# Alternating column halves in the last heads' values, 28 masks on ACT, tau loaded apart, and a new plan

## The chip, the cores and the metric

The kernel runs on one core of a Trainium2 chip. The metric is the device time of one execution in microseconds. The engines are named as in the profile: PE (TensorE; PEld is its weight load), DVE (VectorE), ACT (ScalarE), POOL (GpSimd) and SP (SyncE, which issues DMAs here).

## The reference

An attention with a threshold, then two feed-forward layers on its output. Attention has 4 batches, 8 heads, 576 positions and 64 columns a head; each layer has 2304 tokens, 512 columns and 2048 inner columns.

```python
scores = scale * np.matmul(q, k.transpose(0, 1, 3, 2))
thresh = np.max(scores, axis=-1, keepdims=True) - tau
scores = np.where(scores >= thresh, scores, -1000000000.0)
scores = scores - np.max(scores, axis=-1, keepdims=True)
attn = np.exp(scores)
attn = attn / (np.sum(attn, axis=-1, keepdims=True) + 1e-09)
return np.matmul(attn, v).astype(np.float32)
...
r = np.maximum(h, 0.0)      # first layer: g = r * r, h = x @ w_in
g = h * np.tanh(sp)         # second layer: sp = log(1 + exp(h))
return (g @ w_out).astype(np.float32)
```

The weights of both layers come as 64-bit floats, which the kernel reads as pairs of 32-bit words.

## The kernel before, in words

The work is a list of operations (`op`, `dma`), each with the engines that may do it, an estimated duration on each, what it reads and writes, and a due time. `Plan.order` then lays them out with a model of the engines (`forwards`, `backwards`), and the kernel is issued in the order of the starts that this gives. The table `PAR` holds the due times and the choices of buffers; `LOADS` holds the estimated issue and transfer times of each kind of DMA. What an engine does, and in which order, is therefore fixed before the run; on the chip each engine takes its own list in order and waits on semaphores.

Attention goes through the 4 batches in turn, each as 4 pairs of heads. A pair has 576 query positions: four units of 128 queries with two heads each (`hh` 0 and 1), and a last unit of 64 queries, in which the two heads share the 128 partitions (`hh` = 2: head 0 in partitions 0 to 63, head 1 in 64 to 127). A unit computes scores on PE (`unit`, `scores`), on DVE the scaled scores with their minimum (`top`, L882), the threshold (`most`, L892), on ACT the exponential (`weigh`, L908), and on DVE the mask (`mask`, L919), which multiplies the exponentials with "score within the threshold" and sums them up in `l`. So nine heads are weighed a pair, if the last unit counts as one. Then the weights are turned and multiplied with the values.

There are kinds of pairs. Kind d (all four of batch 0, one of batch 1) works in float32: PE turns the weights (`values_direct`, L991), ACT copies them out, PE multiplies (two heads alternate in `turned`; the last unit's `values` does one head after the other). Kinds h and s (the other 11 pairs) split the weights into two f16 parts, turn them by DMA (`transpose`, tile pt), and multiply with two f16 parts of the values in `values` of `head`, L956 to L962: 14 matmuls a head.

Weights of the first layer (`weights`) are rewritten to two float32r parts each: on ACT a scaling (L525), on ACT or DVE a shift of the lower word (L537 or L544), on DVE a clamp (L532) and two bit operations (L549, L555), the upper part on ACT or DVE (L583), the lower part on DVE (L594). This runs beside the attention of batches 0 and 1, in places of buffers that the planner lends. The first layer's blocks (`first_part`: tiles h and acc) run between the units of later batches; the second layer comes last.

At the start one operation, `consts`, makes the identity, loads tau and does three small DVE operations with it; everything that reads the identity or these numbers depends on it in the plan. `warm` puts single 128-column matmuls (`spin`) into PE's early idle time, in three groups.

Of the kernel before, what the change touches and what calls it, by code (L numbers as in the profile page):

```python
# [16 lines left out]
AF = mybir.ActivationFunctionType  # L17
ALU = mybir.AluOpType
# [8 lines left out]
PAR = dict(  # L27
    on=dict(),
    merge=8,
    warm=(1, 3, 7),  # L30
    won=("S", "S"),
    land=2.419,
    lag=0.518,
    turns=("h", "s1"),
    kv=(("nat0", "V1"), ("f1", "nat1"), ("KT1", "f0"), ("V0", "KT0")),
    cd=(-150.532, 10.911, -114.568),
    urg=-5.54,
    rawt=23.548,
    kinds="dddd",
    cgen=1.383,  # L40
    split=(),
    ex=dict(cw=1, cr=6, raw=17, pd=2, sc=3),
    exo=("cw", "pd", "sc", "cr", "raw"),
    blk=list((17.026, 77.25, 181.004, 262.558, 368.796, 471.734, 577.967, 790.694, 936.347)),
    tb2=145.883,
    down2=89.229,
    sp=(0, 0),
    off=(170.46, 68.826, 37.695, -205.928, 58.656, 43.101, -191.105, -38.461),
    ahead=(10.872, 128.518, 9.367, -61.853, 3.491, 155.716, -16.749, 483.826, 162.488, -31.72),
    start=-197.714,  # L50
    area=dict(sc=("x0", "x1"), hl=("x2",)),
    jobahead=19.381,
    fbi=6,
    stay=1.0,
    stayt=150.0,
    kinds2="ssss",
    kb=("dhss", "ssss", "ssss"),
)

# [21 lines left out]
class Plan:  # L81
# [5 lines left out]
    TABLE = 1.3  # L87
    BIAS = {"V": 1.26, "A": 0.34, "P": 3.463, "S": 0.46}
    SHARE = 0.8
# [238 lines left out]
def attention_moe_moe_kernel(ctx: ExitStack, tc: tile.TileContext, q, k, v, tau, w1i, w1o, w2i, w2o, out):  # L328
    nc = tc.nc
    B, H, S, D = q.shape  # L330
# [3 lines left out]
    plan = Plan()  # L334
    op = plan.op
# [68 lines left out]
    def rot(*places):  # L404
# [9 lines left out]
        "q1": (dict(S=0.75, P=0.8), 0.0, 0.4, 0.4), "q2": (dict(S=1.45, P=1.4), 0.62, 0.19, 0.65),  # L414
        "w8": (dict(S=0.65, P=0.9, A=0.5), 0.0, 3.5, 3.45),
        "w": (dict(S=0.6, P=0.75, A=0.45), 0.0, 1.8, 1.75), "n3": (dict(S=2.3, P=2.0), 1.24, 0.9, 1.6),
        "n2": (dict(S=1.45, P=1.35), 0.62, 0.5, 1.4),
        "xs": (dict(S=0.72, P=0.65), 0.0, 0.36, 0.36), "tail": (dict(S=1.6, P=1.3), 0.6, 0.19, 0.38),
        "xl": (dict(S=0.63, P=0.56), 0.0, 0.55, 0.5), "x2": (dict(S=0.6, P=0.56), 0.0, 0.75, 0.7),
        "xr": (dict(S=0.45, P=0.56), 0.0, 0.64, 0.64), "out": (dict(S=0.45, A=0.45), 0.0, 0.65, 0.65),  # L420
        "out2": (dict(S=1.3), 0.6, 0.2, 0.5), "turn": (dict(S=1.55), 0.0, 1.3, 1.2),
    }
# [11 lines left out]
    def mm(o, l, r, start, stop):  # L434
        nc.tensor.matmul(o, l, r, start=start, stop=stop, skip_group_check=True)  # L435
# [11 lines left out]

    K, K0 = plan.buf("const", lambda: None), plan.buf("ones", lambda: None)
    op({"P": 0.5}, lambda e: nc.gpsimd.memset(ones, 1.0), w=[K0], due=-60.0)

    def consts(e):
        make_identity(nc, ident)
        nc.sync.dma_start(out=tt[:, 3:4], in_=tau.to_broadcast([128, 1]))

        nc.vector.tensor_scalar(
            out=tt[:, 0:1], in0=tt[:, 3:4], scalar1=0.0, scalar2=-0.125, op0=ALU.is_ge, op1=ALU.mult
        )
        nc.vector.tensor_scalar(out=tt[:, 1:2], in0=tt[:, 3:4], scalar1=0.0, scalar2=None, op0=ALU.max)

        nc.vector.tensor_copy(out=cd[:, 3:4], in_=tt[:, 0:1])  # L460

    op({"S": 0.5}, consts, w=[K], due=-50.0, load=(0.0, 0.7, 0.7))


    W = {}
# [159 lines left out]
    def pow2(name, raws, junk, due):  # L625
# [23 lines left out]
        t = pbuf(place("s", "s0", "s1"), [128, 1024])  # L649
        op({"T": 0.22}, lambda e: mm(t()[:, 0:n], ones, mx(), True, True), r=[mx, K], w=[t], due=due + 0.1)  # L650

# [104 lines left out]
    turns = []  # L756
# [17 lines left out]
    def job_direct(p, due):  # L774
# [10 lines left out]
        for x, dst, z, (j0, j1) in todo:  # L785
# [23 lines left out]

            t = op({"T": 0.15 * (j1 - j0)}, turn, r=[raw, K], w=[o], due=due - z)  # L810
            if len(turns) < 2:
# [33 lines left out]
    def unit(p, g, hh, j, due):  # L845
# [9 lines left out]
        def scores(e):  # L855
# [13 lines left out]

        op({"T": (1.2 if direct else 0.85) if hh < 2 else 0.65 if direct else 0.48}, scores, r=[QT, KT], w=ss, due=due,  # L870
           half=3 if direct else 2)
# [33 lines left out]
    def weigh(p, hh, j, i, sc, m, nt, due):  # L905
        ex = sbuf(place("e", "e0", "e1"), [128, 576], F32)
        op({"A": 0.67},
           lambda e: nc.scalar.activation(  # L908
               out=ex(), in_=sc(), func=AF.Exp, bias=m()[:, i:i + 1], scale=-1.0),
           r=[sc, m], w=[ex], due=due + 1.5 - URG, tab=("exp", "ln"))  # L910
# [12 lines left out]

        op({"V": 0.74}, mask, r=[sc, nt], x=[ex], w=[l], due=due + 2 - URG, two=True)

        return u, ex

    def head(p, g, hh, u, ex, due):
# [26 lines left out]
        def values(e):  # L955
            for h in ((hh,) if hh < 2 else (0, 1)):  # L956
                sl = slice(0, 128) if hh < 2 else slice(64 * h, 64 * h + 64)
                for i in range(9):
                    t = 5 * h + (i if i < 5 else i - 5)
                    mm(o()[sl, 64 * u:64 * u + 64], pt()[:, i, sl], V()[:, t, 0:64], i == 0, i == 8)  # L960
                    if i < 5:
                        mm(o()[sl, 64 * u:64 * u + 64], pt()[:, i, sl], V()[:, t, 64:128], False, False)  # L962

        op({"T": 0.41 if hh < 2 else 0.9}, values, r=[pt, V], w=[o], due=due + 7 + O_VA, half=1)
        if last:
            normal(p, g, hh, due)

    def values_direct(p, g, hh, u, ex, last, o, due):
# [23 lines left out]

        op({"T": 0.6}, turn, r=[ex, K], w=ts, due=due + 2.5 + O_DIR)
        if not p.late:
# [115 lines left out]
    def attention(b, groups, t0, t1, tails):  # L1110
        n = NPR * (4 * len(groups) + tails)
        i = 0
        for pr in range(NPR):
# [62 lines left out]
    def x_first(n, due):  # L1176
        xh, xo = sbuf("xh", [128, 2, 4, 128], F32R), sbuf("xo", [128, 2, 4, 128], F32R)
        o = pbuf(rot("s0", "s1"), [128, 1024])
        for t in range(2):
            for g in range(2):  # L1180
# [315 lines left out]
```

## Time and profile before

| | us |
|---|---|
| median of 3 runs | 1029.93 (1028.37 to 1031.53) |
| the profiled execution | 1031.52 |
| its span | 1029.7 |
| PE busy | 1002.4 |
| DVE busy | 617.9 |
| ACT busy | 622.0 |

The span runs from the first to the last instruction; the rest of an execution's time lies around it. Busy time of PE is by modelled ends, since matmuls are pipelined. The page's second part cuts the span into 40 equal slices; a digit is the busy share in tenths, and PEclk the granted clock in tenths of full speed.

### The profile page before, as it was taken

What the parts mean: (1) busy time and instruction counts of PE and PEld (TensorE: products, weight loads), DVE (VectorE), ACT (ScalarE), POOL (GpSimd) and SP (SyncE); (2) the same over time, 40 slices, a digit from 0 to 9 for tenths busy, and PEclk for the clock granted to TensorE, in tenths of its full rate; (3) what the DMA queues carried; (4) which work ended last, traced back from release to release, by engine and by line L of the source; (5) the groups of instructions that cost most, each with busy time, mean ns of one, the idle gap of its engine ahead of it and who ended that gap; (6) DMA issues with size and microseconds to landing.
All of it is one profiled execution on the core that took longest, in us unless ns stands there. A gap on an engine that the chain in (4) does not pass through costs nothing.

```text
span 1029.7 us, 21534 instructions
## 1 busy us (share of the span) xinstructions
PE 1002.4 (97%) x8581; PEld 888.2 (86%) x8581; DVE 617.9 (60%) x1442; ACT 622.0 (60%) x1143; POOL 0.8 (0%) x7
## 2 busy tenths in 40 slices
PE   5999999999999999999999999999999999999997
PEld 4666789889888998889999999988888888888897
DVE  5999999998899887989765137971211211211111
ACT  5989999777787877877576459962322332232231
POOL 0000000000000000000000000000000000000000
PEclk9999999999999999999999999999999999999999
DMA  9732247798788988887674123521100110010010
GB/s 286 207 112 86 87 139 146 156 157 174 164 164 150 163 158 172 149 156 137 138 204 149 42 68 108 196 91 30 45 8 1 41 41 1 21 41 1 1 41 21
DMA packets 231188, 109.48 MB, mean 106 GB/s; under 512 B 194608, under 2 KB 212016, under 8 KB 231088
## 3 DMA queue, kind: packets, MB, share of 16 engines
q1 hardware_dynamic: 230816, 107.98, 44.8%
q8 instruction: 67, 1.10, 0.4%
q14 instruction: 33, 0.27, 0.1%
q10 hardware_dynamic: 272, 0.13, 0.0%
HBM read 58.16 MB, written 14.16 MB: 70 GB/s over the span
## 4 chain that ended last, share of the span: by engine, by line
PE 83%; ACT 5%; DMA 5%; DVE 4%; SPq 2%; issue 1%; ACTq 0%; DVEq 0%
PE acc L435 26%; PE s L435 22%; PE h L435 21%; PE small L435 10%; DMA pt<-hl 2%; DMA area<-in_moe_w_in_dram 2%; ACT e L908 1%; SPq L792 1%; DMA f<-in_q_dram 1%; DMA area<-in_moe_w_out_dram 1%; DVE e L919 1%; PE s L1187 1%; PE h L991 0%; PE acc L991 0%; ACT stg L525 0%
## 5 line engine op out<-in xcount | busy, mean ns | idle before, releaser
L435 PE MATMUL acc<-gh,wo 128*128 128x256 f32 x1152 | 215.4, 280 | 0.0
L435 PE MATMUL h<-xh,wi 128*128 128x256 f32 x1152 | 213.2, 279 | 0.8 <-ACT r L1232 0.5
L435 PEld LDWEIGHTS h<-xh,wi 128*128 128x128 f32 x1152 | 182.4, 192 | 4.7 <-issue 1.6
L435 PEld LDWEIGHTS acc<-gh,wo 128*128 128x128 f32 x1152 | 183.0, 192 | 3.8 <-issue 3.0
L435 PE MATMUL h<-xo,wi 128*128 128x256 f32 x576 | 158.4, 275 | 0.0
L435 PE MATMUL acc<-gl,wo 128*128 128x256 f32 x576 | 158.4, 275 | 0.0
L594 DVE TENSOR_TENSOR gl<-r,gh 128x512 fp32r<-128x512 f32 x90 | 62.2, 691 | 157.7 <-ACT gh L583 157.4
L435 PEld LDWEIGHTS acc<-gl,wo 128*128 128x128 f32 x576 | 110.5, 192 | 0.0
L435 PEld LDWEIGHTS h<-xo,wi 128*128 128x128 f32 x576 | 110.5, 192 | 0.0
L435 PE MATMUL s<-KT,area 64*128 64x512 f16 (+7 forms) x840 | 88.3, 333 | 3.9 <-ACT area L817 2.5
L583 ACT ACTIVATE gh<-r 128x512 fp32r<-128x512 f32 x87 | 54.7, 628 | 46.3 <-PE small L435 24.0
L919 DVE SCALAR_TENSOR_TENSOR e<-area,n,e 128x576 f32<-128x576 f32 x93 | 74.9, 815 | 8.9 <-ACT e L908 8.8
L435 PE MATMUL acc<-wo,gh 128*128 128x512 f32 x240 | 79.7, 379 | 0.0
L882 DVE TENSOR_SCALAR_CACHE_REDUCE area<-s,c 128x576 f32<-128x576 f32 x90 | 71.7, 814 | 7.2 <-PE s L435 6.8
L594 DVE TENSOR_TENSOR pt<-area,pt 128x512 fp32r<-128x512 f32 x18 | 12.5, 692 | 102.1 <-ACT pt L583 102.1
L908 ACT ACTIVATE e<-area,m 128x576 f32<-128x576 f32 x93 | 70.0, 765 | 2.7 <-DVE area L948 1.6
L948 DVE TENSOR_TENSOR hl<-e,hl 128x512 f16<-128x512 f32 (+1 forms) x136 | 61.0, 454 | 7.3 <-ACT hl L943 7.2
L1232 ACT ACTIVATE r<-h 128x512 f32<-128x512 f32 x71 | 42.0, 592 | 35.5 <-PE h L435 28.6
L435 PE MATMUL small<-V,pt 128*128 128x64 f16 (+1 forms) x1540 | 58.9, 194 | 2.4 <-DMA pt<-hl 1.7
L435 PEld LDWEIGHTS <-pt 128*128 128x128 f16 (+1 forms) x1540 | 50.4, 101 | 10.1 <-issue 5.9
L943 ACT ACTIVATE hl<-e 128x576 f16<-128x576 f32 x68 | 46.0, 678 | 19.8 <-DVE e L919 10.3
L1282 ACT ACTIVATE r<-s 128x512 f32<-128x512 f32 x17 | 10.2, 601 | 68.4 <-PE s L435 68.4
(306 smaller groups left out, 2050.3 us busy)
## 6 DMA issues: line engine op xcount, KB each, us to landing
area<-in_moe_w_out_dram SPq DMA_DIRECT2D x20, 512.0 KB, 4.1
area<-in_moe_w_in_dram SPq DMA_DIRECT2D x17, 512.0 KB, 3.6
wi<-in_moe_w_in_dram SPq DMA_DIRECT2D x10, 512.0 KB, 4.1
xx<-xdr SPq DMA_DIRECT2D x36, 128.0 KB, 2.6
x2dr<-stg SPq DMA_DIRECT2D x18, 256.0 KB, 3.1
xdr<-xx SPq DMA_DIRECT2D x32, 128.0 KB, 2.2
f<-in_q_dram SPq DMA_DIRECT2D x24, 128.0 KB, 3.1
V<-in_moe_w_out_dram SPq DMA_DIRECT2D x6, 512.0 KB, 4.1
```

The source lines that it names most:

```text
L435: nc.tensor.matmul(o, l, r, start=start, stop=stop, skip_group_check=True)
L583: nc.scalar.activation(out=o, in_=i, func=AF.Copy)
L594: VEC[e].tensor_tensor(out=part(lo), in0=src(), in1=f32(part(hi)), op=ALU.subtract)
L792: e.dma_start(out=raw()[:, j0:main, h, :], in_=x[h, 0:512, :].rearrange("(p j) d -> p j d", j=4)[:, j0:main, :],)
L882: nc.vector.tensor_scalar(out=sc(), in0=s()[:, 0:576], scalar1=c()[:, 3:4], scalar2=None, op0=ALU.mult, op1=ALU.min, accum_out=m()[:, i:i ...
L908: lambda e: nc.scalar.activation(out=ex(), in_=sc(), func=AF.Exp, bias=m()[:, i:i + 1], scale=-1.0),
L919: nc.vector.scalar_tensor_tensor(out=ex(), in0=sc(), scalar=nt()[:, i:i + 1], in1=ex(), op0=ALU.is_le, op1=ALU.mult, accum_out=l()[:, 0, u ...
L943: nc.scalar.activation(out=hl()[:, 0:576], in_=ex(), func=AF.Copy)
L948: VEC[e].tensor_tensor(out=hl()[:, a:a + n], in0=ex()[:, z:z + n], in1=hl()[:, z:z + n], op=ALU.subtract)
L1187: nc.tensor.transpose(o()[:, z + c:z + c + 128], xl()[:, c:c + 128], ident)
L1232: nc.scalar.activation(out=halves(r()), in_=turned_out(ph()), func=AF.Relu)
L1282: nc.scalar.activation(out=out, in_=in_, func=AF.Mish)
```

## The change

Five things are changed.
1. `consts` is split: the identity is an operation of POOL, the load of tau a DMA of its own, and the DVE operations with tau an operation that reads it (one more: minus tau, clipped at 0, in column 5). What needs only the identity or the ones depends on these alone.
2. In the last unit's `values`, of `head` and of `values_direct`, the loop over heads is moved inside the loop over positions, so that matmuls to the two column halves alternate.
3. In `weigh`, for some heads (`pm` counts them by batch), the exponential and the mask are replaced: ACT takes a parametric relu of threshold minus scaled score with a slope of 3e38 for negative arguments, and then an exponential with its sum.
4. Estimated durations and biases of the planner are changed.
5. All due times and the lending of buffers are new.

```diff
-    warm=(1, 3, 7),
+    warm=(1, 0, 7),
...
-    land=2.419,
-    lag=0.518,
-    turns=("h", "s1"),
+    land=1.952,
+    lag=0.652,
+    turns=("h", "s0", "s1"),
...
-    cd=(-150.532, 10.911, -114.568),
-    urg=-5.54,
-    rawt=23.548,
+    cd=(-170.545, 5.765, -140.676),
+    urg=-11.867,
+    rawt=17.065,
...
-    ex=dict(cw=1, cr=6, raw=17, pd=2, sc=3),
-    exo=("cw", "pd", "sc", "cr", "raw"),
-    blk=list((17.026, 77.25, 181.004, 262.558, 368.796, 471.734, 577.967, 790.694, 936.347)),
+    ex=dict(cw=1, cr=2, raw=18, pd=5, sc=5),
+    exo=("cr", "sc", "cw", "pd", "raw"),
+    blk=list((31.54, 89.582, 173.595, 259.276, 365.591, 458.78, 583.659, 811.548, 994.61)),
...
-    stay=1.0,
-    stayt=150.0,
+    stay=1.5,
+    stayt=220.0,
     kinds2="ssss",
     kb=("dhss", "ssss", "ssss"),
+    pm=(1, 5, 0, 1),
...
-    BIAS = {"V": 1.26, "A": 0.34, "P": 3.463, "S": 0.46}
+    BIAS = {"V": 2.37, "A": 1.589, "P": 3.556, "S": 0.46}
...
-        "w8": (dict(S=0.65, P=0.9, A=0.5), 0.0, 3.5, 3.45),
-        "w": (dict(S=0.6, P=0.75, A=0.45), 0.0, 1.8, 1.75), "n3": (dict(S=2.3, P=2.0), 1.24, 0.9, 1.6),
+        "w8": (dict(S=0.65, P=0.9, A=0.5), 0.0, 2.9, 2.8),
+        "w": (dict(S=0.6, P=0.75, A=0.45), 0.0, 1.8, 1.42), "n3": (dict(S=2.3, P=2.0), 1.24, 0.9, 1.6),
...
+        "tau": (dict(S=0.5, P=0.6), 0.0, 0.2, 0.2),
...
-        "out2": (dict(S=1.3), 0.6, 0.2, 0.5), "turn": (dict(S=1.55), 0.0, 1.3, 1.2),
+        "out2": (dict(S=1.3), 0.6, 0.2, 0.5), "turn": (dict(S=1.55), 0.0, 1.3, 1.05),
...
-    K, K0 = plan.buf("const", lambda: None), plan.buf("ones", lambda: None)
+    K, K0, KI, KT_ = (plan.buf(z, lambda: None) for z in ("const", "ones", "ident", "tau"))
     op({"P": 0.5}, lambda e: nc.gpsimd.memset(ones, 1.0), w=[K0], due=-60.0)
+    op({"P": 0.8}, lambda e: make_identity(nc, ident), w=[KI], due=-60.0)
 
     def consts(e):
-        make_identity(nc, ident)
-        nc.sync.dma_start(out=tt[:, 3:4], in_=tau.to_broadcast([128, 1]))
...
+        nc.vector.tensor_scalar(out=tt[:, 5:6], in0=tt[:, 1:2], scalar1=-1.0, scalar2=None, op0=ALU.mult)
         nc.vector.tensor_copy(out=cd[:, 3:4], in_=tt[:, 0:1])
 
-    op({"S": 0.5}, consts, w=[K], due=-50.0, load=(0.0, 0.7, 0.7))
+    dma(lambda e: e.dma_start(out=tt[:, 3:4], in_=tau.to_broadcast([128, 1])), "tau", w=[KT_], due=-40.0)
+    op({"V": 0.45}, consts, r=[KT_], w=[K], due=-39.0)
...
+        p.n += 1
+        if p.n * PAR["pm"][p.b] % 9 < PAR["pm"][p.b]:
+            def cut(e):
+                nc.scalar.activation(
+                    out=ex(), in_=sc(), func=AF.Prelu, bias=nt()[:, i:i + 1], scale=-1.0, alpha=3e38)
+
+            def exp(e):
+                nc.scalar.activation(
+                    out=ex(), in_=ex(), func=AF.Exp, bias=tt[:, 5:6], accum_out=l()[:, 0, u:u + 1])
+
+            op({"A": 0.67}, cut, r=[sc, nt], w=[ex], due=due + 1.5 - URG, tab=("exp", "ln"))
+            op({"A": 0.76}, exp, r=[K], x=[ex], w=[l], due=due + 1.9 - URG, tab=("exp", "ln"))
+            return u, ex
...
-            for h in ((hh,) if hh < 2 else (0, 1)):
-                sl = slice(0, 128) if hh < 2 else slice(64 * h, 64 * h + 64)
-                for i in range(9):
-                    t = 5 * h + (i if i < 5 else i - 5)
-                    mm(o()[sl, 64 * u:64 * u + 64], pt()[:, i, sl], V()[:, t, 0:64], i == 0, i == 8)
-                    if i < 5:
-                        mm(o()[sl, 64 * u:64 * u + 64], pt()[:, i, sl], V()[:, t, 64:128], False, False)
-
-        op({"T": 0.41 if hh < 2 else 0.9}, values, r=[pt, V], w=[o], due=due + 7 + O_VA, half=1)
+            for i in range(9):
+                for z in range(0, 128 if i < 5 else 64, 64):
+                    for h in ((hh,) if hh < 2 else (0, 1)):
+                        sl = slice(0, 128) if hh < 2 else slice(64 * h, 64 * h + 64)
+                        t = 5 * h + i % 5
+                        mm(o()[sl, 64 * u:64 * u + 64], pt()[:, i, sl], V()[:, t, z:z + 64],
+                           i == 0 and z == 0, i == 8)
+
+        op({"T": 0.41 if hh < 2 else 0.55}, values, r=[pt, V], w=[o], due=due + 7 + O_VA, half=1)
...
-            for h in (0, 1):
-                sl = slice(64 * h, 64 * h + 64)
-                for i in range(5):
-                    d = slice(0, 128) if i < 4 else slice(64, 128)
+            for i in range(5):
+                d = slice(0, 128) if i < 4 else slice(64, 128)
+                for h in (0, 1):
+                    sl = slice(64 * h, 64 * h + 64)
                     mm(o()[sl, 64 * u:64 * u + 64], pt()[d, i, sl], V()[d, 5 * h + i, :], i == 0, i == 4)
 
-        op({"T": 1.6}, values, r=[pt, V], w=[o], due=due + 7 + O_VA)
+        op({"T": 1.0}, values, r=[pt, V], w=[o], due=due + 7 + O_VA)
```

## Rows read from the trace of the kernel before

**Rows 1.** The page: busy us, share and instructions of each engine.
```profile
PE 1002.4 (97%) x8581; PEld 888.2 (86%) x8581; DVE 617.9 (60%) x1442; ACT 622.0 (60%) x1143; POOL 0.8 (0%) x7
```
**Rows 2.** Stretches: us, busy us of each engine (instructions), granted clock, DMA share, GB/s.
```profile
0.00:25.00 25.00, 13.68 (x57) 10.31 (x58) 13.90 (x32) 12.96 (x23) 0.84 (x7) 0.97 0.93 286
20.00:30.00 10.00, 8.35 (x59) 5.87 (x58) 9.02 (x22) 8.14 (x17) 0.00 (x0) 0.83 1.10 325
25.00:175.00 150.00, 143.53 (x1279) 109.25 (x1278) 145.35 (x370) 138.39 (x286) 0.00 (x0) 0.99 0.48 131
25.00:235.00 210.00, 201.82 (x2014) 161.62 (x2013) 202.56 (x519) 186.65 (x377) 0.00 (x0) 1.00 0.58 138
200.00:1020.00 820.00, 816.67 (x6942) 744.02 (x6943) 432.92 (x980) 449.19 (x795) 0.00 (x0) 1.00 0.43 96
```
**Rows 3.** Timeline of PE at 125 us: start, us, instructions.
```profile
125.14 0.38 PE L435 MATMUL h<-xh,wi 128*128 128x256 f32 x1
```
**Rows 4.** Timeline of the first 9 us: ACT, SP's issue of tau, DVE.
```profile
0.73 1.28 ACT L525 ACT_TABLE_LOAD   x1 [0.73 <-PEq L1478]
...
3.92 0.47 SPq L453 DMA_DIRECT2D tt<-in_tau_dram  x1
4.38 0.66 ACT L525 ACTIVATE wo<-xh 128x512 f32<-128x512 f32 x1 [2.36 <-DMA xh<-in_moe_w_out_dram]
...
8.30 0.66 ACT L525 ACTIVATE stg<-area 128x512 f32<-128x512 f32 x1 [2.72 <-DMA area<-in_moe_w_in_dram]
8.51 0.15 DVE L455 TENSOR_SCALAR tt<-tt 128x1 f32<-128x1 f32 x1 [8.51 <-DMA tt<-in_tau_dram]
...
8.77 0.42 DVE L532 TENSOR_SCALAR wo<-wo 128x512 f32<-128x512 f32 x1
```
**Rows 5.** Groups by line: count, busy us, mean ns of one, idle before.
```profile
L435 PE MATMUL small<-V,pt 128*64 128x64 f16 x308 | 10.7, 197 | 1.6 <-DMA pt<-hl 1.3 <-DVE xx L1067 0.3
...
L435 PE MATMUL small<-V,nat 128*64 128x64 f32 (+1 forms) x20 | 1.8, 231 | 0.0
```
**Rows 6.** Timelines of PE: bursts of the last unit's values.
```profile
48.21 1.80 PE L435 MATMUL small<-V,wo 128*64 128x64 f32 x20
...
162.01 1.80 PE L435 MATMUL small<-V,nat 128*64 128x64 f32 x20
...
230.63 0.94 PE L435 MATMUL small<-V,pt 128*64 128x64 f16 x28 [0.27 <-DVE xx L1067]
```
**Rows 7.** Timeline: direct values of a full unit, heads in turn.
```profile
27.40 0.27 PE L435 MATMUL small<-wo,V 128*64 128x128 f32 x1
...
27.40 0.27 PE L435 MATMUL small<-wi,V 128*64 128x128 f32 x1
...
27.50 0.27 PE L435 MATMUL small<-wo,V 128*64 128x128 f32 x1
```
**Rows 8.** Timeline: neighbouring exponentials and masks; below, the group of ACT's accumulator reads.
```profile
19.47 0.76 ACT L908 ACTIVATE e<-wi,m 128x576 f32<-128x576 f32 x1
...
20.14 0.76 ACT L908 ACTIVATE e<-wo,m 128x576 f32<-128x576 f32 x1
...
22.27 0.81 DVE L919 SCALAR_TENSOR_TENSOR e<-wi,n,e 128x576 f32<-128x576 f32 x1
...
23.00 0.81 DVE L919 SCALAR_TENSOR_TENSOR e<-wo,n,e 128x576 f32<-128x576 f32 x1
...
L638 ACT ACTIVATION_READ_ACCUMULATOR nat<-f 128x1 f32 x19 | 3.6, 189 | 0.0
```
**Rows 9.** Weights' lower word: groups in 0:200 on ACT; line L544 on DVE (min/median/max ns).
```profile
L537 ACT ACTIVATE area<-area 128x512 int32<-128x512 uint32 x16 | 11.7, 734 | 0.0
...
L544 DVE TENSOR_SCALAR wi<-wi x1: 452/452/452, 128.1 to 128.1; 128x512 int32<-128x512 int32 x1
```
**Rows 10.** Stretch of line L919 (masks) alone: DVE busy us (instructions), clock, DMA.
```profile
25.00:175.00 150.00, 39.77 (x98) 0.99 0.48 131
```
**Rows 11.** Timeline of PE ahead of the first scores: spins.
```profile
10.69 2.08 PE L435 MATMUL acc<-ones 128*128 128x128 f32 x8
```

More of the change, by code (lines that the diff above doesn't have):

```diff
@@ L29 @@
     merge=8,
-    warm=(1, 3, 7),
+    warm=(1, 0, 7),
     won=("S", "S"),
-    land=2.419,
-    lag=0.518,
-    turns=("h", "s1"),
+    land=1.952,
+    lag=0.652,
+    turns=("h", "s0", "s1"),
     kv=(("nat0", "V1"), ("f1", "nat1"), ("KT1", "f0"), ("V0", "KT0")),
-    cd=(-150.532, 10.911, -114.568),
-    urg=-5.54,
-    rawt=23.548,
+    cd=(-170.545, 5.765, -140.676),
+    urg=-11.867,
+    rawt=17.065,
     kinds="dddd",
-    cgen=1.383,
+    cgen=3.036,
     split=(),
-    ex=dict(cw=1, cr=6, raw=17, pd=2, sc=3),
-    exo=("cw", "pd", "sc", "cr", "raw"),
-    blk=list((17.026, 77.25, 181.004, 262.558, 368.796, 471.734, 577.967, 790.694, 936.347)),
-    tb2=145.883,
-    down2=89.229,
+    ex=dict(cw=1, cr=2, raw=18, pd=5, sc=5),
+    exo=("cr", "sc", "cw", "pd", "raw"),
+    blk=list((31.54, 89.582, 173.595, 259.276, 365.591, 458.78, 583.659, 811.548, 994.61)),
+    tb2=86.684,
+    down2=75.393,
     sp=(0, 0),
-    off=(170.46, 68.826, 37.695, -205.928, 58.656, 43.101, -191.105, -38.461),
-    ahead=(10.872, 128.518, 9.367, -61.853, 3.491, 155.716, -16.749, 483.826, 162.488, -31.72),
-    start=-197.714,
+    off=(198.434, 66.485, 14.577, -170.54, 59.272, 47.202, -206.707, -25.553),
+    ahead=(13.109, 65.307, 9.335, -144.435, 7.693, 138.195, 9.734, 513.856, 144.95, 10.325),
+    start=-200.781,
     area=dict(sc=("x0", "x1"), hl=("x2",)),
-    jobahead=19.381,
-    fbi=6,
-    stay=1.0,
-    stayt=150.0,
+    jobahead=18.556,
+    fbi=7,
+    stay=1.5,
+    stayt=220.0,
     kinds2="ssss",
     kb=("dhss", "ssss", "ssss"),
+    pm=(1, 5, 0, 1),
 )
@@ L649, in pow2 @@
         t = pbuf(place("s", "s0", "s1"), [128, 1024])
-        op({"T": 0.22}, lambda e: mm(t()[:, 0:n], ones, mx(), True, True), r=[mx, K], w=[t], due=due + 0.1)
+        op({"T": 0.22}, lambda e: mm(t()[:, 0:n], ones, mx(), True, True), r=[mx, K0], w=[t], due=due + 0.1)
         ts = nc.vector.tensor_scalar
@@ L808, in turn @@
                     )
-            t = op({"T": 0.15 * (j1 - j0)}, turn, r=[raw, K], w=[o], due=due - z)
+            t = op({"T": 0.15 * (j1 - j0)}, turn, r=[raw, KI], w=[o], due=due - z)
             if len(turns) < 2:
@@ L868, in scores @@
                         mm(o[:, c0:c1], l, r, i == 0, i == (0 if direct else 2))
-        op({"T": (1.2 if direct else 0.85) if hh < 2 else 0.65 if direct else 0.48}, scores, r=[QT, KT], w=ss, due=due,
+        op({"T": (1.2 if direct else 0.85) if hh < 2 else 1.0 if direct else 0.76}, scores, r=[QT, KT], w=ss, due=due,
            half=3 if direct else 2)
@@ L906, in weigh @@
         ex = sbuf(place("e", "e0", "e1"), [128, 576], F32)
[L907 to L910, printed above, removed]
         u = 2 * hh + j if hh < 2 else 0
@@ L916, in weigh @@
         l = p.l
+        p.n += 1
[9 more added lines that the diff above has]
+            return u, ex
+        op({"A": 0.67},
+           lambda e: nc.scalar.activation(
+               out=ex(), in_=sc(), func=AF.Exp, bias=m()[:, i:i + 1], scale=-1.0),
+           r=[sc, m], w=[ex], due=due + 1.5 - URG, tab=("exp", "ln"))
         def mask(e):
@@ L991, in turn @@
                 nc.tensor.transpose(part(i), ex()[:, z:z + 128], ident)
-        op({"T": 0.6}, turn, r=[ex, K], w=ts, due=due + 2.5 + O_DIR)
+        op({"T": 0.6}, turn, r=[ex, KI], w=ts, due=due + 2.5 + O_DIR)
         if not p.late:
@@ L1056, in turned @@
         op({"A": 0.2, "V": 0.22}, evac, r=[ot], w=[xt], due=due + 0.5)
-        op({"T": 0.14}, lambda e: nc.tensor.transpose(o()[:, 128 * j:128 * j + 128], xt(), ident), r=[xt, K], w=[o], due=due + 1)
+        op({"T": 0.14}, lambda e: nc.tensor.transpose(o()[:, 128 * j:128 * j + 128], xt(), ident), r=[xt, KI], w=[o], due=due + 1)
     def normal(p, g, hh, due):
@@ L1117, in attention @@
             p.tiles = (2 * groups[0], 5 if tails else 2 * groups[-1] + 2)
-            p.keep = None
+            p.keep, p.n = None, -1
             p.late = b > 0 or 0 not in groups
@@ L1187, in turn @@
                         nc.tensor.transpose(o()[:, z + c:z + c + 128], xl()[:, c:c + 128], ident)
-                op({"T": 0.218}, turn, r=[xl, K], w=[o], due=due - 0.5)
+                op({"T": 0.218}, turn, r=[xl, KI], w=[o], due=due - 0.5)
             def part(y, t=t):
```

## The prediction, made before the result was known

> **What bounds the kernel now.** I began with the page's busy shares: PE is busy 1002.4 of 1029.7 us, DVE and ACT 60% each [rows 1]. The whole span alone says "PE"; the table of stages says where [rows 2]. From 200 to 1020 us PE is busy 816.7 of 820 us, and DVE and ACT little more than half. PE time taken out there comes off the end one for one. Earlier it is different. From 25 to 175 us PE is busy 143.5 of 150 us by its modelled ends, but DVE is busy 145.4 and ACT 138.4. This stretch holds the attention of batch 0, part of that of batch 1, and the rewriting of the first layer's weights; matmuls of the first layer appear only from 125.1 us [rows 3]. There DVE is the tightest engine, with ACT close behind. Before that, DVE does nothing for 8.51 us, and the wait is put down to the DMA of tau [rows 4].
>
> So the change can pay in two ways: in PE time after about 125 us, and in DVE time before it, which brings the first layer's matmuls forward.
>
> **Tail values in f16.** There are 11 pairs of heads of kind h or s; 308 matmuls, 28 each [rows 5]. One burst of 28 starts at 230.63 and lasts 0.94 us [rows 6]; less the 0.19 us (mean 197 ns) that one matmul takes [rows 5], 27 steps cost 0.75 us, 28 ns a step. At present the 14 matmuls of head 0, which fill columns 0 to 63, go ahead of the 14 of head 1; afterwards they alternate. That neighbours on different halves run side by side is seen in the direct values, where two heads alternate already: two matmuls start at 27.40 and the next pair at 27.50, so a pair costs what one would [rows 7]. Fourteen steps in place of 28 would save 0.39 us; if the loads of the two halves queue, nothing. I take 0.35, close to what rows 7 show: 11 x 0.35 = 3.9 us, between 0 and 4.3.
>
> A rule of the Trainium skill speaks against this: TensorEngine Tiling (Array Packing), section Restrictions and Gotchas, says that column tiling and the fast weight load exclude each other, and TensorE: Matmul & The Clock Gate, section LDWEIGHTS, prices a load at its number of columns divided by 1.2 in ns, an estimated 53 ns for 64. By it, with loads one by one, a burst of 28 could not take less than some 1.5 us and the 3.9 us would be 0. The trace disagrees on the price at least: 28 of them now take 0.94 us [rows 6].
>
> **Tail values in f32.** There are 5 pairs of kind d, with 20 records a burst; a burst takes 1.80 us [rows 6]. A record takes 0.23 us by the mean of its group [rows 5], so 19 steps cost 1.57 us; alternating halves them, and two of the four changes between whole and half depth go: 0.8 us saved a burst, between 0 and 1.0. Four of the five bursts lie before 125 us, where DVE sets the pace, and I count them as nothing (3.2 us if PE sets it). The fifth, at 162.01, stands among the first layer's matmuls and counts: 0.8. Tails together: 4.7 us.
>
> **Masks.** pm = (1, 5, 0, 1) takes head 0 of each pair of batches 0 and 3, and the heads counted 0, 2, 4, 6 and 8 (of nine) of each pair of batch 1: 4 + 20 + 4 = 28. Each takes one scalar_tensor_tensor and its accumulator read from DVE; two that follow each other start at 22.27 and 23.00, so one frees 0.74 us [rows 8]. On ACT the exponential becomes a parametric relu of the same shape, and a second exponential with an accumulator is new. Two exponentials start 0.67 us apart [rows 8], and the accumulator's read takes 0.19 in the rows of the squares: 0.86 us more. No row shows the relu; I give it the exponential's price, as the same form on the same engine, between 0.64 (the 0.73 us of a copy of 512 columns [rows 9], less the same overlap) and 0.86 us: 28 x (-0.03 to +0.19). The relu waits for the threshold, a small operation that ACT has ahead of its exponential already, so no wait is new; what stands behind a late relu on ACT is weight work, which DVE waits for.
>
> From 25 to 175 us DVE runs 49 masks (98 instructions with the reads [rows 10]); with the two before, 36 are of batch 0 and 15 of batch 1. Of the 28 that move, 4 + 8 = 12 are among them. DVE loses 8.9 us and ACT gains 10.3: 136.5 against 148.7 of 150, which ACT cannot hold with any wait. But the planner may put the shift of the weights' lower word on either: 0.73 us on ACT, 0.45 on DVE [rows 9], or 0.64 and 0.38 where neighbours overlap. Moving 11.8 of them levels both engines at 141.0 us, where DVE had 145.4. So the exchange is worth 4.4 us of that stretch, not 8.9. Two thirds of the stretch (25 to 125 us) lie before the first layer's matmuls fill PE: I count 2.9 us. Above, 5.9 (all of DVE's); below, a loss, since ACT may keep everything (in the rivals). The other 16 masks lie where PE has no room: nothing.
>
> **Tau apart.** Three tiny operations at the head of DVE's queue wait for a DMA issued at 3.92. The first weight tile was ready for DVE at 5.04, when ACT's first copy ended, and DVE took it at 8.77 [rows 4]. Without the wait DVE gains up to 3.7 us; but the second tile leaves ACT at 8.96, and DVE idles 2.6 us between 8.5 and 25 as it is (25 - 8.5 - 13.9 [rows 2]). I take 1.5, between 0 and 3.7. If tau's issue moves back on SP, q's loads behind it go out 0.47 us sooner. Should tau come late, the first minimum waits for it, and on DVE the weights behind it.
>
> **Warming.** Three of eleven spins go; those between the two sets of transposes and the first scores start at 10.69, while PE waits for ACT [rows 11]: nothing, unless the clock suffers. The granted clock is 0.83 in 20 to 30 us even with them, which lies between its two levels, 1.2 and 2.4 GHz [rows 2]; a longer stretch at the lower one costs at most some 2 us, as PE is busy 13.7 of the first 25 us.
>
> **The rest of the plan**: new due times, places (cr 6 to 2, pd 2 to 5, sc 3 to 5), a third PSUM place for the turned heads, lower prices for weight loads and transposes. PE idles 6.5 us from 25 to 175 and 3.3 from 200 to 1020: a better order can win some 10 us, a worse one lose as much. With no row for either, 0.
>
> **Sum.** 4.7 + 2.9 + 1.5 = 9.1 us. The profiled execution took 1031.5 us, its span 1029.7 and 1.8 around it; the median of the runs is 1029.9. I take the saving from the median: 1020.8 us.
>
> **Rivals.**
> Only the tails pay: ACT, 92% busy in 25 to 175 us, leaves the planner no way to use DVE's free time, and the first layer begins as late as now: 1029.9 - 4.7 = 1025.2. For it, ACT has only 11.6 us idle there; against it, weight work that can move. 20%.
>
> Nothing pays: the halves do not overlap in f16 and the early gain is eaten: 1029.9. Against it stand the pairs of rows 7. 11%.
>
> ACT becomes the bound, and it gets slower: the 10.3 us stay on ACT in 25 to 175 us while it keeps its idle share of 7.7%, much of which is waiting. The stretch grows by 10.3 / 0.923 = 11.2 us; less tails and tau (6.2), 1034.9. It decides once more than 6.2 x 0.923 = 5.7 us of the 10.3 stay there. For it: ACT is the second tightest engine by 7 us only. 10%.
>
> The parametric relu needs another table: the trace has one table load ahead of all exponentials, 1.28 us [rows 4]. Two loads a mask are 56, of which the 48 of batches 0 and 1 (61 us) fall where ACT is idle some 23 us (25 to 235 us [rows 2]): about 40 us late, 1070. 3%.
> The Trainium skill, ScalarE: Activation LUTs, section What ACT_TABLE_LOAD costs, adds a drain and says 2.66 us a switch, an estimated 149 us for 56; no row here shows the drain.
>
> The better plan fills PE's idle time as well: another 9 us or so, 1012. 6%.
>
> **How the numbers follow.** The forecast, 1015 to 1025, has 50%. 0.3% is about 3.1 us, what a measurement can tell from no change: under 1026.8 is faster. Forecast, tails alone and the better plan make 76% faster; 11% the same; the two slow cases 13%. The range, 1012 to 1031, leaves out the slow ones and half of the best.
>
> **What would show it.** A burst of 28 in 0.6 us or less and an f32 burst near 1.0, with single records as long as now. 116 masks on DVE, 28 relus near 0.77 us on ACT. DVE's first operation near 5 us. The first matmul on xh some 4 us ahead of 125.1, and PE full from there. It is wrong if bursts keep their length, if ACT goes over 95% in 25 to 175 us while DVE idles for its exponentials, if table loads appear, or if PE idles anew after 200 us on transfers that the lower prices ask for too late.

## The result, and the profile after

The changed kernel takes 1015.9 us (median of 4, 1014.8 to 1019.6), the kernel before 1029.15 in the same comparison. The ratio is 0.9874, with an interval of 0.9843 to 0.9905: 13.2 us less, where 9.1 were forecast. The profiled execution took 1016.4 us, with a span of 1014.6; that of before lay 2.3 us above its median, so the two traces differ by 15.1. Of these, 9.6 us are busy time of PE and 5.5 its idle time.

The busy line of the page after, beside [rows 1]: PE loses 9.6 us of work, DVE 14.0; ACT gains 9.4, and POOL has work now.
```profile
PE 992.8 (98%) x8575; PEld 879.0 (87%) x8575; DVE 603.9 (60%) x1395; ACT 631.4 (62%) x1178; POOL 12.1 (1%) x20
```
The stretches after (columns as in [rows 2]):
```profile
0.00:25.00 25.00, 18.36 (x90) 12.79 (x92) 14.38 (x38) 15.40 (x29) 0.85 (x7) 1.00 0.91 241
20.00:30.00 10.00, 9.28 (x86) 6.91 (x84) 10.00 (x27) 10.00 (x24) 0.00 (x0) 1.00 1.06 250
25.00:175.00 150.00, 144.34 (x1352) 110.69 (x1353) 143.94 (x356) 143.33 (x303) 8.33 (x10) 1.00 0.52 144
25.00:235.00 210.00, 201.97 (x2092) 162.73 (x2093) 198.71 (x494) 197.01 (x411) 10.46 (x12) 1.00 0.64 150
200.00:1000.00 800.00, 797.75 (x6812) 727.45 (x6811) 420.88 (x944) 446.74 (x795) 1.65 (x2) 1.00 0.44 97
```
The column of the clock prints 1.00 also where the trace holds no clock record. The first record is at 13.5 us here and at 19.9 us in the kernel before; ahead of it PE's transposes of 128 columns start 0.21 us apart, later 0.11, so PE ran at its lower level there.

Against [rows 2], DVE and ACT are now level (198.7 and 197.0 in 25 to 235 us), PE is busy 4.7 us more by 25 us, and late in the span it is as full as it was. The first matmul on xh comes 8.8 us sooner, and the end 15.1: by these two traces more than half of the gain is made early. Of the other 6 us, about half are the short f16 bursts (11 x 0.31 = 3.4). Where the gain arises shows in the timelines. First PE, against [rows 3] and [rows 6]: the first matmul on xh, and the bursts.
```profile
47.25 0.95 PE L437 MATMUL small<-V,wi 128*64 128x64 f32 x20
...
116.31 0.38 PE L437 MATMUL h<-xh,wi 128*128 128x256 f32 x1
...
222.10 0.63 PE L437 MATMUL small<-V,pt 128*64 128x64 f16 x28
```
The groups of the tails, against [rows 5]: single matmuls last as long as before.
```profile
L437 PE MATMUL small<-V,pt 128*64 128x64 f16 x308 | 7.0, 197 | 1.1 <-DVE xx L1082 1.1
```
The masks on ACT, against [rows 8]: timeline, and below it the groups of the new instructions.
```profile
14.30 0.76 ACT L929 ACTIVATE e<-wi,m 128x576 f32<-128x576 f32 x1
14.96 0.76 ACT L918 ACTIVATE e<-wi,n 128x576 f32<-128x576 f32 x1
...
17.23 0.76 ACT L922 ACTIVATE e<-e,tt 128x576 f32<-128x576 f32 x1
17.90 0.19 ACT L922 ACTIVATION_READ_ACCUMULATOR e<-e,tt 128x1 f32 x1
...
L922 ACT ACTIVATE e<-e,tt 128x576 f32<-128x576 f32 x28 | 21.7, 776 | 0.1
...
L918 ACT ACTIVATE e<-area,n 128x576 f32<-128x576 f32 x15 | 11.6, 770 | 0.2
...
L922 ACT ACTIVATION_READ_ACCUMULATOR e<-e,tt 128x1 f32 x28 | 5.5, 196 | 0.0
```
The relu costs what an exponential costs, and none of them loads a table.

The start, against [rows 4]. The new plan issues k and q of the first pair ahead of tau and the weights; DVE's queue still begins with tau and waits until 8.40.
```profile
0.74 1.38 SPq L794 DMA_DIRECT2D wo<-in_k_dram  x2
...
2.83 1.28 SPq L794 DMA_DIRECT2D wi<-in_q_dram  x2
...
4.83 0.59 SPq L464 DMA_DIRECT2D tt<-in_tau_dram  x1
5.47 0.43 SPq L502 DMA_DIRECT2D xh<-in_moe_w_out_dram  x1
...
8.40 0.15 DVE L455 TENSOR_SCALAR tt<-tt 128x1 f32<-128x1 f32 x1 [8.40 <-DMA tt<-in_tau_dram]
...
10.91 0.43 DVE L534 TENSOR_SCALAR wi<-wi 128x512 f32<-128x512 f32 x1 [2.04 <-ACT wi L527]
```
Attention comes first and the weights later. Two marks of DVE's timeline show it: the last minimum of the first pair, and the 16th bit operation of the first layer's weights. Before:
```profile
37.21 0.81 DVE L882 TENSOR_SCALAR_CACHE_REDUCE wo<-s,cd 128x576 f32<-128x576 f32 x1
...
42.17 0.69 DVE L555 SCALAR_TENSOR_TENSOR stg<-wo,stg 128x512 int32<-128x512 int32 x1
```
After:
```profile
27.92 0.82 DVE L884 TENSOR_SCALAR_CACHE_REDUCE wo<-s,cd 128x576 f32<-128x576 f32 x1
...
58.51 0.66 DVE L557 SCALAR_TENSOR_TENSOR stg<-area,stg 128x512 int32<-128x512 int32 x1
```
Attention is 9.3 us ahead, the weights 16.3 us late. Counted on in the same way, the 32nd, 48th and 64th of these operations are 8.5, 4.4 and 3.4 us late, while the pairs keep a lead of 7 to 14 us.

### The profile page after: what moved, and what is told of

The parts are those of the page before. It is cut to its first block, busy times and chain, and to the rows that moved or that the text cites. A ratio compares the mean times of both kernels' runs of the same rounds, so it can differ in the third digit from the quotient of the medians.

```text
span 1014.6 us, 21490 instructions
## 1 busy us (share of the span) xinstructions
PE 992.8 (98%) x8575; PEld 879.0 (87%) x8575; DVE 603.9 (60%) x1395; ACT 631.4 (62%) x1178; POOL 12.1 (1%) x20
## 4 chain that ended last, share of the span: by engine, by line
PE 74%; DVE 4%; DMA 3%; ACT 2%; issue 1%; SPq 0%; ACTq 0%; DVEq 0%
PE acc L437 26%; PE s L437 20%; PE h L437 20%; PE small L437 8%; DMA pt<-area 2%; DVE area L884 1%; PE s L1202 1%; DMA area<-in_moe_w_out_dram 1%; DMA pt<-hl 0%; DVE hl L963 0%; DVE gl L596 0%; DVE area L963 0%; DVE stg L551 0%; DVE e L934 0%; ACT hl L958 0%
## 5 line engine op out<-in xcount | busy, mean ns | idle before, releaser
L934 DVE SCALAR_TENSOR_TENSOR e<-area,n,e 128x576 f32<-128x576 f32 x76 | 61.2, 815 | 11.0 <-ACT e L929 10.2
L963 DVE TENSOR_TENSOR hl<-e,hl 128x64 f16<-128x64 f32 (+1 forms) x135 | 59.8, 456 | 4.6 <-ACT hl L958 4.5
L929 ACT ACTIVATE e<-area,m 128x576 f32<-128x576 f32 x76 | 57.3, 765 | 0.9 <-DVE area L963 0.6
L437 PE MATMUL small<-V,pt 128*128 128x64 f16 (+1 forms) x1540 | 54.7, 194 | 1.4 <-DVE xx L1082 1.1
L437 PEld LDWEIGHTS <-pt 128*128 128x128 f16 (+1 forms) x1540 | 46.5, 101 | 10.0 <-issue 7.7
L437 PEld LDWEIGHTS acc<-wo,gh 128*128 128x128 f32 x240 | 45.4, 189 | 7.5 <-ACT area L1404 1.1
L437 PE MATMUL s<-f,wi 128*128 128x512 f32 (+1 forms) x160 | 50.0, 358 | 0.0
```

Of the source, the lines that this page charges most:

```text
L929: lambda e: nc.scalar.activation(out=ex(), in_=sc(), func=AF.Exp, bias=m()[:, i:i + 1], scale=-1.0),
L934: nc.vector.scalar_tensor_tensor(out=ex(), in0=sc(), scalar=nt()[:, i:i + 1], in1=ex(), op0=ALU.is_le, op1=ALU.mult, accum_out=l()[:, 0, u ...
L963: VEC[e].tensor_tensor(out=hl()[:, a:a + n], in0=ex()[:, z:z + n], in1=hl()[:, z:z + n], op=ALU.subtract)
```

## The experiments

"Order kept" means that the instructions keep the order that the plan of that kernel gave; "replanned" that the planner worked it out anew.

**1. The halves alone, in the kernel before, order kept.**
```diff
-            for h in ((hh,) if hh < 2 else (0, 1)):
-                for i in range(9):
...
+            for i in range(9):
+                for z in range(0, 128 if i < 5 else 64, 64):
+                    for h in ((hh,) if hh < 2 else (0, 1)):
```


> The kernel before with the matmuls of the last unit's values alternating between the column halves, and nothing else: prices, plan and every engine's order as before. Theory (the tails count where PE has no room): a burst of 28 falls from 0.94 to some 0.6 us, an f32 burst from 1.80 to some 0.95; eleven bursts and one f32 burst pay, 4.4 us less than before, between 3.5 and 5. Rival (PE waits elsewhere for what the bursts gave, or the halves queue): less than 1.5 us.

Measured: 1024.31 against 1029.29, ratio 0.9953 (0.994 to 0.9965), -4.8 us by the ratio. The theory holds.

**2. The halves undone, in the kernel after, order kept** (the same edit the other way).

> The changed kernel with the old loop order in both values, the plan and every other order as changed. Theory: 4 to 5 us slower than the changed kernel, 8.5 to 9.5 us faster than before. Rival (the plan leans on the shorter bursts, so that late values hold up copies and more): 7 us or more slower than the changed kernel.

Measured: 1021.04, ratio to before 0.9928 (0.9916 to 0.9941): 5.1 us more than after by the medians, 5.6 by the ratios. The two experiments agree: the tails are worth about 5 us.

**3. 28 masks on ACT in the kernel before, order kept.**
```diff
+            if cut:
+                nc.scalar.activation(
+                    out=ex(), in_=sc(), func=AF.Prelu, bias=nt()[:, i:i + 1], scale=-1.0, alpha=3e38)
+                nc.scalar.activation(
+                    out=ex(), in_=ex(), func=AF.Exp, bias=tt[:, 5:6], accum_out=l()[:, 0, u:u + 1])
+                return
```


> The kernel before with the 28 masks of the change on ACT: no operation at the place of their exponential, and relu and exponential at the place of their mask; plan and all other orders as before. Theory (DVE sets the pace before the first layer's matmuls fill PE, and ACT has a little room): the first layer begins 1 to 3 us earlier and the time falls by 1 to 3 us, less than the forecast's 2.9 as nothing is moved from ACT in return. Rival (ACT becomes the bound): ACT above 95% in 25 to 175 us, 1 to 6 us slower.

Measured: 1041.73, ratio 1.0117 (1.0104 to 1.0131): 12.0 us slower. DVE's longest waits in 25 to 235 us, in total us, number of waits and the longest:
```profile
DVE e L932 <- ACT e L914: 8.3, 8, 2.1
DVE hl L961 <- ACT hl L956: 5.8, 7, 1.4
```
and one of the stretches in which time is lost:
```profile
150.00:175.00 25.00, 23.45 (x218) 20.93 (x216) 20.06 (x48) 24.34 (x50) 0.00 (x0) 1.00 0.65 152
```
ACT is busy 24.3 of 25 us, and DVE, at 20.1, waits there for other work of ACT: 2.6 us for the copies ahead of `hl`, 1.4 for a scaled weight. Of the 8.3 us for exponentials, 6.2 lie from 175 to 235 us. The last minimum of a pair falls back from 0.0 us at the fourth pair (107 us) to 8.1 at the eighth (248 us in the kernel before). So the rival "ACT becomes the bound" is real when nothing moves in return, and costs twice the 6 us expected, although ACT is at 94.2% in 25 to 175 us.

**4. The masks back on DVE in the kernel after, order kept.** One of the 28 stays on ACT, because its buffers are used again too soon; the exponential's bias is the threshold, which the normalisation cancels.
```diff
+                if no not in stay:
+                    nc.vector.scalar_tensor_tensor(
+                        out=ex(), in0=sc(), scalar=nt()[:, i:i + 1], in1=ex(), op0=ALU.is_le, op1=ALU.mult,
+                        accum_out=l()[:, 0, u:u + 1],
+                    )
```


> The changed kernel with 27 of the 28 masks back on DVE: exponential at the relu's place, mask at the place of the second exponential (one stays, as its buffers are used again too soon); plan and all other orders as changed. Theory: DVE gets 27 x 0.74 = 20 us back, about 9 of them before 175 us; with two thirds of that ahead of the full PE, 4 to 8 us slower than the changed kernel, 5 to 9 faster than before. Rival (the masks' engine does not matter, the gain is the order at the start): under 2 us slower than the changed kernel.

Measured: 1027.18, ratio to before 0.9978 (0.9968 to 0.9989), 11.3 us above after by the medians, 10.7 by the ratios: more than the 4 to 8 expected. Where the buffers would be used again too soon, a mask stands earlier than the second exponential did. In the trace the last minimum of each pair lags behind that of after by 0.5, 1.2, 2.0, 2.7 us in batch 0 (one mask a pair), by 3.9, 6.2, 11.2, 11.2 in batch 1 (five a pair) and by 11.2 at the last pair of batch 3. So 8.5 us are lost in batch 1, 5.0 of them between the last minima of its second and third pair (178 to 206 us after, 184 to 217 here), while its fourth pair and batch 3's four masks cost nothing. The clock was granted at 0.50 from 199.8 to 203.2 us in this trace, so up to 1.7 of the 5.0 us can be the clock's. The stretch from 175 to 200 us, the kernel before:
```profile
175.00:200.00 25.00, 23.94 (x288) 20.96 (x286) 25.00 (x62) 20.30 (x38) 0.00 (x0) 1.00 0.77 148
```
after:
```profile
175.00:200.00 25.00, 22.70 (x286) 20.29 (x286) 23.59 (x61) 23.99 (x50) 1.29 (x1) 1.00 0.77 157
```
and with the masks back on DVE:
```profile
175.00:200.00 25.00, 21.98 (x266) 18.79 (x265) 24.87 (x56) 19.90 (x38) 1.28 (x1) 1.00 0.79 164
```
DVE is full there in the kernel before and in this one, and not after.

**5. Tau's three operations just ahead of the first minimum, in the kernel before.**
```diff
+    pend = []
+
+    def with_tau():
...
+                while pend:
+                    pend.pop()()
```


> The kernel before with the three small DVE operations on tau put just ahead of the first minimum, the load of tau and all other orders as before. The prediction's step: DVE starts at about 5 us in place of 8.5 and 1.5 us is gained in all (0 to 3.7). Rival, from the changed kernel's trace, where DVE waits for tau to 8.40 as before: DVE's next work waits for ACT and loads anyway, 0 to 0.5 us.

Measured: 1027.35, ratio 0.9986 (0.9977 to 0.9995), 1.4 us faster (0.5 to 2.4), as the prediction's step says. DVE now starts on the weights:
```profile
4.94 0.43 DVE L537 TENSOR_SCALAR wo<-wo 128x512 f32<-128x512 f32 x1 [4.94 <-ACT wo L530]
```

**6. The new parameters alone**: no masks, old loops at their old prices, replanned.
```diff
-    pm=(1, 5, 0, 1),
+    pm=(0, 0, 0, 0),
```


> The changed kernel's parameters, prices and split of the identity from tau, planned anew with all masks on DVE and the old loops in both values (with their old prices 0.9 and 1.6). Theory (tails 5, masks some 4, the rest 4): 1023 to 1027 us, 2 to 6 faster than before. Rival (the new plan is nearly all of what is not tails): 1019 to 1022 us. Second rival (the parameters fit only the new operations): slower than before.

Measured: 1028.95, ratio 0.9996 (0.9987 to 1.0005): nothing, which none of the three expectations said. The first pair is 4.6 us ahead, but the weights' four marks are 15.9, 13.6, 13.5 and 11.1 us late, and the first matmul on xh is no sooner (125.4).

**7. The first pair's k and q loads first on SP, in the kernel before, all other orders kept.**
```diff
+            early.append(len(plan.ops))
...
+    seq = early[:2] + [n for n in seq if n not in early[:2]]
```


> The kernel before with the loads of the first pair's keys and queries put first on SP's queue, all other orders as before. Theory (the changed kernel's start comes from the order of the loads): the first transposes start at 4.4 in place of 5.7 us and the first scores some 3 to 5 us earlier, 1 to 4 us gained in all. Rival (ACT's and DVE's orders, with weight work ahead, set the start): the weight work waits longer, 0 or slower by up to 2 us.

Measured: 1032.98, ratio 1.0041 (1.0028 to 1.0053), slower by 4.2 us, twice what the rival allowed. PE turns k and q sooner, but DVE's first weight waits until 12.20 and, with ACT's weight work ahead of it in the old order, the first pair is 3.1 us late too.
```profile
4.50 1.38 PE L807 MATMUL s<-ident,wo 128*128 128x128 f32 x5 [2.71 <-DMA wo<-in_k_dram]
...
12.20 0.42 DVE L532 TENSOR_SCALAR wo<-wo 128x512 f32<-128x512 f32 x1
```

**8. All edits with the old parameters** (due times, places and biases of before), replanned.
```diff
-    BIAS = {"V": 2.37, "A": 1.589, "P": 3.556, "S": 0.46}
+    BIAS = {"V": 1.26, "A": 0.34, "P": 3.463, "S": 0.46}
```


> All edits of the change with the parameters and biases of before (the prices of operations and loads as changed), planned anew. Theory: tails 5 and the better part of masks and tau: 1020 to 1024 us. Rival (the gain beyond the tails needs the new parameters): 1024 to 1028 us.

Measured: 1021.16, ratio 0.9912 (0.9898 to 0.9925), -9.1 us, within the theory's range.

**9. The kernel after without its eight spins.**
```diff
-        z = 128 * (i % 8)
+        return
```


> The changed kernel without its eight warming matmuls, every other order as changed. First theory (spins stand ahead of the first scores on PE, which could start at 8.7 in place of 9.5 us): 0.5 to 1 us faster than the changed kernel. Second (they keep PE's clock up): the granted clock falls in the first 30 us, the early scores take longer, 1 to 4 us slower than the changed kernel. The prediction's step (spins lie where PE waits): no difference.

Measured: 1017.4, ratio 0.9883 (0.9869 to 0.9896), not told apart from after. The clock's column prints 1.00 from 0 to 30 us, but the first clock record of this trace is at 22.8 us, against 13.5 after, and PE's rows show the lower level ahead of it. Four transposes without the spins:
```profile
19.57 1.11 PE L1006 MATMUL h<-ident,e 128*128 128x128 f32 x4
...
23.74 0.65 PE L1006 MATMUL h<-ident,e 128*128 128x128 f32 x4
```
and after:
```profile
18.27 0.66 PE L1006 MATMUL h<-ident,e 128*128 128x128 f32 x4
```
So the second theory has its premise: PE runs some 9 us longer at the lower level. The price is small: the last minimum of the first pair is 2.1 us later than after, that of the last pair 0.3, and the span ends 0.8 us later.

**10. POOL's work on DVE, in the kernel after, order kept.**
```diff
-            o.fn(o.eng)
+            o.fn("V" if o.eng == "P" and "V" in o.opts else o.eng)
```


> The changed kernel with the 13 operations that its plan put on POOL done by DVE at the same place, every other order as changed. Theory (DVE sets the pace up to about 235 us, and what is taken off it comes off the end): nine clamps at some 0.38 us, two lower parts at 0.62 and two small ones are 5 us more on DVE, 2 to 5 us slower than the changed kernel. Rival (POOL's work was off the chain, and slow there): within 1 us.

Measured: 1016.96, ratio 0.9876 (0.9863 to 0.989), not told apart from after. My theory of 2 to 5 us was wrong; what POOL took over is not on the path. Its groups in the kernel after:
```profile
L534 POOL TENSOR_SCALAR stg<-stg 128x512 f32<-128x512 f32 x8 | 5.7, 715 | 113.5 <-ACT stg L527 113.5
L596 POOL TENSOR_TENSOR wo<-stg,wo 128x512 fp32r<-128x512 f32 x2 | 2.9, 1462 | 49.8 <-ACT wo L585 49.8
```

**11. The masks alone with the old parameters**, replanned (the edit of experiment 3, as operations of the plan).

> The kernel before with the 28 masks of the change on ACT and its own parameters, planned anew; neither tails nor tau. Theory (all edits under the old parameters gave 8.6 us, tails 5 and tau 1.4 of it by their own runs): 1 to 4 us faster than before. Rival (the run with all edits owes more to masks than the sum says, as the old plan also moves work from ACT): 5 us or more faster. Second rival, from the run with the orders kept: slower than before.

Measured: 1029.46, ratio 1.0005 (0.9994 to 1.0015): nothing, where 1 to 4 us were expected. The weights' second and third marks are 10.0 and 7.5 us sooner, and the first seven pairs are within 2 us of where they were.

**12. The kernel after without masks on ACT**, replanned (pm all 0, the halves kept).

> The changed kernel with all masks on DVE, tails alternating, its own parameters, planned anew. Theory (the plan cannot make up for the masks under these parameters; the plan alone gave 0.8, tails 5): 1022 to 1026 us, 6 to 10 slower than the changed kernel. Rival (most of the masks' worth with orders kept, 11 us, is that the order does not fit, and a new plan recovers it): 1016 to 1021 us.

Measured: 1023.74, ratio 0.9942 (0.9928 to 0.9955): 7.0 us short of after by the ratios, as the theory says. The last minima of the pairs lag behind those of after by 0.6, -0.6, -0.7 and 2.0 us in batch 0, by 1.6, 3.7, 5.6 and 4.5 in batch 1. DVE and the clock around 185 us:
```profile
180.00:182.00 2.00, 0.92 (x9) 0.82 (x8) 2.00 (x4) 1.35 (x3) 0.00 (x0) 1.00 0.79 175
182.00:184.00 2.00, 0.69 (x4) 0.16 (x5) 2.00 (x6) 1.54 (x4) 0.00 (x0) 0.94 0.65 138
184.00:186.00 2.00, 1.68 (x18) 0.88 (x15) 2.00 (x4) 1.32 (x3) 0.00 (x0) 0.50 0.96 220
...
183.74:193.98 10.24, 9.49 (x75) 5.99 (x75) 10.24 (x26) 7.25 (x16) 0.00 (x0) 0.50 0.74 159
```
DVE is full, PE stands idle for 2.4 of 4 us, waiting for DVE's minima among others, and then the clock is granted at 0.50, its lower level of 1.2 GHz, until 194. The mean clock of all five executions was 0.994 to 0.996, against 0.999 to 1.00 in three of the four of after (the fourth, at 0.995, took 1019.6 us). Against after, the span is 7.0 us longer: 4.4 of it is busy time of PE for the same 8575 matmuls, and 2.6 idle time. The lower clock explains the 4.4, by an estimate from the last row: half of 9.49 us, or 4.7. What the clock cost the span by itself isn't separated, for DVE was full in that stretch too, and a faster PE might have waited for it.

Put together, in us against the kernel before, by the ratios (with an asterisk where the order was kept):

| | neither | halves | masks | both |
|---|---|---|---|---|
| old parameters | 0 | -4.8* | +0.5 | -9.1 |
| new parameters | -0.4 | -6.0 | -7.4* | -13.0 |

All cells of the lower row, and the last of the upper, have tau and the identity apart as well. With the new parameters the halves bring 5.6 us with or without the masks, and the masks 7.0 with or without the halves; with the old ones the masks alone bring nothing. The interval of after alone is 3.2 us to either side (experiments 9 and 10, near to it, have 1.4), so what is told from that cell is no sharper; experiments 2 and 6, which give the masks' 7.0 without it, have 1.3 and 0.9. Each cell is one order that the planner gave: how much another order of the same cell would differ was not run.

## Why the prediction was right, and where its terms were off

The sign and the two main mechanisms, tails and masks, were as forecast; tau's was not. 1015.9 lies at the low end of the forecast's own 1015 to 1025, 4.9 us below the time named. Of these, 0.8 us is the kernel before, which took 1029.15 in this comparison and not 1029.9. By the table's ratios the rest is the masks, 4.1 us more than forecast, and the tails, 0.9 more, while tau and the rest of the plan brought 1.1 less (0.4 in experiment 6 for 1.5). Step by step:

**Tails: forecast 4.7, measured 4.8 to 5.6.** The two terms were off in opposite directions. An f16 burst went from 0.94 to 0.63 us, 0.31 in place of 0.35: 11 x 0.31 = 3.4 at most. By the trace's single records a step was 31 to 32 ns, not 28, and the first matmuls of head 1 already ran beside the last of head 0 in the kernel before, so less was left to overlap. An f32 burst went from 1.80 to 0.95, 0.85 each or 4.3 for five, of which only the one after 125 us was counted (0.8). PE's busy time fell by 7.7 us in experiment 1, as 3.4 + 4.3 say, and 4.8 (3.6 to 6.2) reached the end. The time alone doesn't tell whether the four early bursts counted, for 3.4 + 0.85 lies within. The trace of experiment 1 says that they did in part, though DVE set the pace there: its first pair is 1.2 us ahead of before, its first matmul on xh 2.7, and the four bursts with their 3.4 us lie between. The rule of the Trainium skill, TensorEngine Tiling (Array Packing), section Restrictions and Gotchas, that was weighed against this term did not cost it: 28 loads and matmuls in column halves took 0.63 us, far below the estimate of 1.5 from the Trainium skill's price of a load.

**Masks: forecast 2.9, measured 7 with the new parameters.** This is the term that was mis-sized. The price of one was right: on ACT the relu stands in the exponential's place with 0.66 us from the start of its neighbour, the second exponential takes 0.67 to its read, and the read 0.19, so 0.86 is added. What failed is the sentence "the other 16 masks lie where PE has no room: nothing". Four of them, batch 3's, are indeed worth nothing in experiment 4, and so are those of batch 1's fourth pair. But with its third pair 5.0 of the 11.2 us are lost. In experiment 12, replanned, at most 2.0 us are lost by the last minimum of the fifth pair (at 130 us after), and the forecast had its 2.9 ahead of that; 3.7 are lost by that of the sixth (at 182 us, before the clock falls) and 5.6 by that of the seventh. PE is busy 23.9 of 25 us from 175 to 200 in the kernel before, and I read that as "no room". But DVE is busy 25.0 of 25 there. My reading, which experiment 4 bears out in its lags, is that PE filled its waits with matmuls of the first layer while DVE still set when attention could go on. I had cut the stretch at 175 us, because [rows 2] showed DVE near its limit up to there, and never looked behind it, although [rows 2] give DVE 202.56 - 145.35 = 57.2 of the 60 us from 175 to 235. The 11 us of experiment 4 are an upper end, as that order was made for masks on ACT; replanned it is 7.

**Levelling.** I expected 11.8 shifts of the lower word to move from ACT to DVE and both engines at 141.0 us of 150. None moved; the shifts on ACT are 31 before 200 us in both kernels. Instead seven copies of an upper part went to DVE, where none was before, and nine clamps from DVE to POOL. ACT instead took 4.9 us more in that stretch (143.3 of 150, which I had thought hard to hold), and DVE, at 143.9, did more work in it. ACT was busy 95.6% without holding DVE up: DVE's waits for the exponentials ahead of its masks total 8.3 us from 25 to 235 us in experiment 3, and 1.6 after. The slow rival is avoided by the order: with the old one kept the masks cost 12.0 us, replanned with the same old parameters 0 (experiment 11).

**Tau: forecast 1.5, measured 1.4 in experiment 5, but not by this way in the kernel after.** There DVE still waits for tau until 8.40, and for its first weight until 10.91. The sign that the prediction named for this term, DVE's first operation near 5 us, did not come. Tau lies in the shade of the late weights, and that a term of 1.5 us stands in a sum that came out in its range is luck.

**The rest of the plan: forecast 0.** Alone it is 0 (experiment 6), as the masks alone are with the old parameters (experiment 11). Together they give 7. The new parameters bring attention forward and pay with 11 to 16 us of the weights, both through DVE; with the masks off DVE the weights catch up until they are 3.4 us late. I had treated two edits that share one engine's time as a sum. Experiment 7 shows the same from the other side: one piece of the new order, put into the old, costs 4.2 us.

**Warming: forecast 0**, not told apart from 0 with all spins gone, although PE then stays longer at the lower clock (experiment 9). **Table loads:** the trace after has two in its whole length as before, one at the start and one ahead of the second layer; that rival is out.

**Open.** Experiment 8 is 4.3 us better than the halves alone, where masks (0) and tau (1.4) alone explain less; whether the split of the identity or the chance of the plan makes the rest was not separated. How much of the 7 us is the lower clock seen in experiment 12 isn't either; it is not all of it, for experiments 6 and 2 differ by 7.0 us too, and in their traces the clock falls early (from 17.6 to 24.5 and from 17.5 to 27.7 us) and otherwise only in the last microseconds. That DVE sets the pace from 175 to 200 us is read from its busy time and the lags; no run relieves DVE in that stretch alone. The 2.3 us by which the profiled execution of before lies above its median, with the clock at 0.83 from 20 to 30 us [rows 2], are no part of the 13.2. No kernel run here beat the changed one.

## What to carry to other kernels

"PE is 96% busy, so nothing can be gained there" is not a safe reading: look, in slices as short as the stage, at whether another engine is full, for that one sets when the next piece may go. Two edits that free and spend the same engine's time can each be worth nothing and together a lot, so test them as a two-by-two table, replanned. The exchange of work between engines paid here only with a new order; with the old one it cost 12 us. And look at what a column prints where its trace has no record: single rows of the engine can settle it.

## What the runs showed of the hardware

- Matmuls of 64 columns on alternating column halves run in pairs in f16 too: 28 in 0.63 us against 0.94, with each still 197 ns long (a step between two of one half is 31 to 32 ns); in f32, 20 in 0.95 against 1.80.
- ACT's parametric relu on 128x576 takes 0.77 us, as the exponential, and shares its table; the accumulator's read adds 0.19.
- POOL takes 0.715 us (mean of eight; a ninth took 1.01) for the clamp of 128x512 that DVE does in 0.42, and 1.46 for the difference of two tiles that takes DVE 0.69.
- With eight spins in PE's early idle time the first record of the full clock is at 13.5 us, without them at 22.8, and the two times are not told apart (ratios 0.9874 and 0.9883).
